# Two of three column blocks of the first expert, computed from the rows of the first 18 chunks by tasks of the attention's planner

## The chip, the cores and the metric

The kernel runs on one core of one Trainium2 chip. Its engines are TensorE (PE, with weight loads shown apart as PEld), VectorE (DVE), ScalarE (ACT), GpSimd (POOL) and SyncE (SP), which here only issues DMAs. The metric is the device time of one execution in microseconds. Everything is float32.

## The reference, cut to what matters

A delta-rule attention over 4 batches, 8 heads, 768 steps and 48 dimensions, whose output is the token matrix of a mixture of 8 experts with hash routing. Each token goes to one expert; there are 3072 tokens of 384 numbers, and an expert is two matrices, 384 by 1024 and 1024 by 384.

```python
for t in range(S):
    kt, vt, bt = (k_n[:, :, t], v[:, :, t], beta[:, :, t, None])
    y[:, :, t] = np.einsum('bhd,bhde->bhe', q[:, :, t], state)
    v_old = np.einsum('bhde,bhd->bhe', state, kt)
    state = state + bt[:, :, :, None] * np.einsum('bhd,bhe->bhde', kt, vt - v_old)
...
x = np.ascontiguousarray(attn_out.transpose(0, 2, 1, 3)).reshape(B * S, H * D)
expert_idx = token_ids * np.int64(2654435761) % np.int64(E)
for e in range(E):
    mask = expert_idx == e
    h = np.maximum(x[mask] @ w1[e], 0.0)
    out[mask] = h @ w2[e]
```

## The kernel before, in words

**Attention.** The 768 steps are cut into 24 chunks of 32 (`NU`, `C`); a chunk handles all 4 batches and 8 heads together. For groups of four chunks the kernel transposes keys and queries (`turn`, lines 381 to 395, into the four `KQ` tiles), multiplies them with each other (`gram`), and inverts the triangular systems on DVE (`inverse`, lines 494 to 554: 31 steps of two operations each), whose result `turn_back` transposes into `TU` (line 560). Then the chunks follow one another, because each needs the state S of the one before (`chunk`, line 594): `ask` reads the state with the keys and with the queries (line 581), R is V minus the first answer, `solve` applies the inverse (line 632), ACT copies the result to W (line 646), `update` adds to the state in PSUM (psS, line 653), the copies of `renew` bring S back to SBUF (lines 676 and 678), and `answer` completes y (line 689). `spread_t` and `masks_of` make the operands Tz and MT of a chunk (lines 466 and 472).

The last four chunks (`TAIL`, 20 to 23) are split in two halves of the heads, so that ACT and DVE share their work: there the eight copies of S are four on ACT (psS banks 0 and 1) and four on DVE (banks 2 and 3). Odd chunks of these four build y in PSUM bank z0, even ones in psY.

At a chunk's end ACT copies y to `x_sb` (line 698), and POOL writes its 128 rows to DRAM with an indirect DMA (`store`, lines 702 and 703). Each row goes to a place that is sorted by expert (`slot`), so that an expert's tokens lie one behind the other in `x_dram`.

**Who sets the order.** All attention work is recorded as tasks with a fixed duration, the names they read and write, and their engine (`task`, line 190). `order` (line 223) plays them through with these durations: an engine takes, of the tasks that are ready, the one with the longest chain of work behind it, plus its `boost`; `more` lengthens a chain, `hold` sets an earliest time, and `PATIENCE` tells how long an engine leaves itself idle for a more urgent task. A PSUM bank (`homes`: z0, z1, psX, psY and the four of psS) is given to a job by the same play. The result is written out as each engine's fixed instruction order.

**Routing.** On DVE, from the token ids: the expert of each token, its rank, the counts of each expert, and for every column block the rows to gather (`rows_i`), which of them are void (`none_f`), and a list of overflow blocks (`ov_i`), all in `routing` (line 717; its operations appear as line 728). The eight experts are sorted by their counts. An expert's own column blocks number `KTS` and hold `CWS` tokens each; what is over is done block by block in the last loop (line 1145). The inputs give no overflow block, before or after: the expert of place 4 has 376 tokens, 282 of them in the first 18 chunks.

**Experts.** They run in the order `RANKS`, place 4 first, which has three columns of 126. For a column, POOL gathers 128 rows (`gather`, line 1017), PE transposes them (`turn`, line 1036), DVE copies the result to xT (line 1038) and makes the token numbers (`token`, lines 1026 and 1028). `gemm1` (line 1044) makes eight blocks of h for all columns of an expert together, whose relu ACT and DVE take in turn (lines 1047 and 1049). `gemm2` (line 1060) makes the output of one column for experts with three columns; experts with four use `gemm2_turned` (line 1078) and turn the result back during the next expert's gemm1 (`send`, line 1088). The columns of the next expert are turned between. POOL scatters the output rows (line 1067).

Weights are 3 MB an expert. The first expert's are loaded in parts from SP behind the stores of the last chunks (lines 90 and 92); those of the next expert are issued from ACT after the first relu of each expert (`between`, lines 80 and 82).

## Time and profile before

Three runs took 538.76, 539.34 and 542.36 us, the median 539.34. The profile is one further execution:

| | |
|---|---|
| profiled execution | 532.51 us |
| its span, from first to last instruction | 530.9 us |
| PE busy | 476.5 us (90%) |
| DVE, ACT, POOL busy | 241.4, 185.9, 95.9 us |
| mean granted TensorE clock | 0.96 of full |
| DMA moved | 59.75 MB |

Stages: attention until about 234 us, then a seam of some 12 us, the experts from 246 to 520, and 11 us after the last scatter (519.7). Numbers of the profile are microseconds from the span's start, and durations are microseconds unless marked ns. A line of a timeline has start, length, engine, source line, operation, output and input tiles with their sizes, how many records were merged (x), and in brackets how long the engine had been idle before, and what it waited for. A window's line gives busy time for each engine, the clock granted to TensorE as a share of full speed, and the DMA engines' share and rate. Tile names are shown without buffer numbers. An f32 matmul leaves two records, a transpose one.

### The profile page before, as it was taken

Reading aid. Unit: us, or ns where it says so; the run is one execution under the profiler, and the core shown is the slowest. Engines: PE = TensorE matmul, PEld = TensorE weight load, DVE = VectorE, ACT = ScalarE, POOL = GpSimd, SP = SyncE. Lnnn points to the kernel's source line nnn. Section 1 sums busy time; section 2 is a strip of 40 time slices with the busy share of each in tenths; the row PEclk is TensorE's granted clock in tenths of the full one; section 3 lists DMA queues with packets and bytes.
Section 4 is the critical chain, followed back from the end, with each engine's and each line's share of the span. In section 5 each row is a group of like instructions: output and inputs, shape, how many; then the busy total and the mean of one; then the engine's idle time right before and its main releaser. Section 6 shows DMA issues by size and latency. Waiting matters only on the chain. (4 is left out here: it accounts for less than half of the span.)

```text
span 530.9 us, 15751 instructions
## 1 busy us (share of the span) xinstructions
PE 476.5 (90%) x6688; PEld 318.1 (60%) x6688; DVE 241.4 (45%) x775; ACT 185.9 (35%) x406; POOL 95.9 (18%) x139
## 2 busy tenths in 40 slices
PE   8865999998998898856999999999999999999990
PEld 5654677777777776643554555555655556565650
DVE  7697899998989886513110111211311111111100
ACT  4634779979796775320101101001011010101100
POOL 7000011021101122127013111302303021102010
PEclk9977899999999899986999999999999999999996
DMA  9959857575333437414705307107144071330000
GB/s 143 167 88 141 133 107 144 116 147 114 79 84 69 90 82 217 133 49 124 261 29 207 117 23 262 56 20 269 55 144 154 28 260 38 130 135 29 14 28 16
DMA packets 119128, 59.75 MB, mean 113 GB/s; under 512 B 104203, under 2 KB 112615, under 8 KB 119057
## 3 DMA queue, kind: packets, MB, share of 16 engines
q1 hardware_dynamic: 103664, 22.04, 23.5%
q10 hardware_dynamic: 10272, 22.14, 11.7%
q0 software_dynamic: 5120, 14.56, 7.9%
q8 instruction: 53, 0.87, 0.7%
q14 instruction: 19, 0.15, 0.1%
HBM read 49.90 MB, written 10.42 MB: 114 GB/s over the span
## 5 line engine op out<-in xcount | busy, mean ns | idle before, releaser
L1044 PE MATMUL h_ps<-xT,w_sb 128*128 128x378 f32 (+3 forms) x384 | 131.5, 496 | 4.0 <-DVE h_sb L1049 3.3
L1044 PEld LDWEIGHTS h_ps<-xT,w_sb 128*128 128x128 f32 x384 | 72.4, 192 | 56.0 <-issue 16.8
L1049 DVE TENSOR_SCALAR h_sb<-h_ps 128x378 f32<-128x378 f32 (+3 forms) x32 | 18.0, 563 | 151.6 <-PE h_ps L1044 151.6
L1078 PE MATMUL oT_ps<-h_sb,w_sb 128*128 128x424 f32 (+1 forms) x192 | 68.0, 507 | 0.0
L1060 PE MATMUL o_ps<-w_sb,h_sb 128*126 128x384 f32 (+1 forms) x192 | 63.6, 486 | 0.0
L546 DVE TENSOR_TENSOR tmp<-U,Ni 128x112 f32<-128x112 f32 (+15 forms) x186 | 61.6, 338 | 3.1 <-ACT U L530 0.4
L544 DVE TENSOR_TENSOR U<-U,tmp 128x112 f32<-128x112 f32 (+15 forms) x186 | 61.6, 338 | 3.0
L1067 POOL DMA_INDIRECT out_dram<-o_sb,idx_i x28 | 27.6, 986 | 194.1 <-ACT o_sb L1066 143.6
L703 POOL DMA_INDIRECT x_scratch<-x_sb,slot x24 | 25.0, 1043 | 193.7 <-DVE U L544 58.3
L1078 PEld LDWEIGHTS oT_ps<-h_sb,w_sb 128*128 128x128 f32 x192 | 35.5, 190 | 25.6 <-issue 13.9
L1047 ACT ACTIVATE h_sb<-h_ps 128x378 f32<-128x378 f32 (+3 forms) x32 | 15.8, 495 | 98.6 <-PE h_ps L1044 98.6
L1060 PEld LDWEIGHTS o_ps<-w_sb,h_sb 128*126 128x126 f32 (+1 forms) x192 | 35.0, 186 | 23.7
L676 ACT ACTIVATE S<-psS 48x384 f32<-48x384 f32 (+1 forms) x92 | 42.6, 463 | 17.4 <-PE psS L653 12.2
L1066 ACT COPY o_sb<-o_ps 126x384 f32<-126x384 f32 (+3 forms) x16 | 7.7, 478 | 83.5 <-PE o_ps L1060 69.0
L1017 POOL DMA_INDIRECT xg<-x_scratch,rows_i x28 | 28.2, 1007 | 34.4 <-DVE idx_i L1028 17.8
L653 PE MATMUL psS<-W,K 32*128 32x96 f32 x736 | 26.9, 280 | 5.8 <-ACT W L646 5.7
L1080 ACT COPY oT<-oT_ps 128x424 f32<-128x424 f32 (+1 forms) x8 | 4.0, 498 | 75.3 <-PE oT_ps L1078 75.3
L689 PEld LDWEIGHTS psY<-W,MT 64*64 64x64 f32 x704 | 23.3, 138 | 10.4 <-issue 9.1
L1038 DVE COPY xT<-xT_ps 128x318 f32<-128x318 f32 (+3 forms) x28 | 14.0, 499 | 33.7 <-PE xT_ps L1036 33.7
L653 PEld LDWEIGHTS psS<-W,K 32*128 32x128 f32 x736 | 22.8, 186 | 9.8 <-ACT W L646 8.3
L689 PE MATMUL psY<-W,MT 64*64 64x48 f32 x704 | 26.6, 225 | 0.0
L581 PE MATMUL psX<-S,KQ 128*32 128x96 f32 x672 | 23.0, 254 | 3.1 <-ACT S L676 2.2
(164 smaller groups left out, 590.9 us busy)
## 6 DMA issues: line engine op xcount, KB each, us to landing
w_sb<-in_moe_w_dram ACTq DMA_DIRECT2D x14, 1536.0 KB
Kt<-in_k_dram SPq DMA_DIRECT2D x24, 192.0 KB
Qt<-in_q_dram SPq DMA_DIRECT2D x24, 192.0 KB
V<-in_v_dram SPq DMA_DIRECT2D x96, 48.0 KB
K<-in_k_dram SPq DMA_DIRECT2D x96, 48.0 KB
w_sb<-in_moe_w_dram SPq DMA_DIRECT2D x3, 512.0 KB
w_sb<-in_moe_w_dram SPq DMA_DIRECT2D x4, 384.0 KB
xg<-x_scratch,rows_i POOLq DMA_INDIRECT x28, 3.0
```

Source lines behind the costliest of these rows:

```text
L544: nc.vector.tensor_tensor(U[:, n:, 0:n], U[:, n:, 0:n], t, op=ALU.add)
L546: nc.vector.tensor_tensor(t, U[:, j:n, 0:n].to_broadcast([P, m, n]), Ni[:, j, n:, None].to_broadcast([P, m, n]), op=ALU.mult)
L581: nc.tensor.matmul(res[quarter(b), u], lhsT=KQ[:, u, a, b, tk], rhs=S0[:, b, u].rearrange("p r d -> p (r d)"), start=(u == first and not o ...
L653: nc.tensor.matmul(psS[:, b, 2 * D * u:2 * D * u + 2 * D], lhsT=K4[quarter(b), u].rearrange("p r d -> p (r d)"), rhs=W[quarter(b), 2 * u:2 ...
L676: nc.scalar.activation(put, get, ACT.Copy)
L689: nc.tensor.matmul(py[rows, h], lhsT=MT[rows, h].rearrange("p e i -> p (e i)"), rhs=W[rows, h], start=(c == 0 and h == 0), stop=True, skip ...
L703: put = nc.gpsimd.indirect_dma_start(out=x_dram[:, :], out_offset=bass.IndirectOffsetOnAxis(ap=slot[:, c:c + 1], axis=0), in_=x_sb, in_off ...
L1017: nc.gpsimd.indirect_dma_start(out=xg, out_offset=None, in_=x_dram[:, :], in_offset=bass.IndirectOffsetOnAxis(ap=rows_i[:, c:c + 1], axis= ...
L1044: nc.tensor.matmul(h_ps[:, :width], lhsT=w1_sb[:, co, fo * P:(fo + 1) * P], rhs=xT[:, co, :width], start=(co == 0), stop=(co == CO - 1))
L1060: nc.tensor.matmul(o_ps[0:rows], lhsT=h_sb[:, fo, col * rows:(col + 1) * rows], rhs=w2_sb[:, fo, :], start=(fo == 0), stop=(fo == FO - 1))
L1067: scat = nc.gpsimd.indirect_dma_start(out=out[:, :], out_offset=bass.IndirectOffsetOnAxis(ap=idx, axis=0), in_=o_sb, in_offset=None, bound ...
L1078: nc.tensor.matmul(oT_ps[:, 0:width], lhsT=w2_sb[:, fo, i * P:(i + 1) * P], rhs=h_sb[:, fo, 0:width], start=(fo == 0), stop=(fo == FO - 1))
```

## The change

- `FIRST` is place 4, the expert that runs first; `SOON` is 18 chunks and `SC` two column blocks.
- **Rows of x in two parts.** Tokens of the first 18 chunks are ranked, by expert, in the first 2304 rows of `x_dram`, the others in the rest. The routing gets further operations: counts of both parts, the distance of an expert's second part from its first (`jump`), and a row number that jumps from one part to the other. Its last task has the priority `more` 75000 in place of 9000.
- **First expert.** The new `first_expert` adds tasks at the end of the list: two loads of its weights on SP; two gathers of 128 rows of the first part on POOL, which depend on the stores of chunks 0 to 17; their transposes, gemm1 for both columns at once (256 wide) and gemm2 on PE; relus and copies on ACT; token numbers on DVE. The PE tasks have a boost of -100000 and are `idle`: the engine waits longer for a more urgent task before it takes one of them. The remaining tokens of the expert, at most 128, form a third column that is done in the old place.
- **Memory.** The tiles `KQ2` and `KQ3` lie in two new tiles `wide`, which later hold the first expert's weights, xT and output; the four `Kt` tiles lie in `keys`, which later holds h.
- **The tail chunks.** y is always in psY, so z0 is free for the new tasks; psX and psS are freed for them after the last W. ACT's and DVE's copies of S are declared independent of each other (S copies freed).
- **Weights.** The second expert's take the place of the first's in the parts behind the last stores; the others are issued one expert earlier for the first three.
- **Built order.** On PE, the transposes of the first background column stand within chunk 20, between the halves of its first `ask`; those of the second column, and all background matmuls, stand behind the `answer` of chunk 23. The two gathers on POOL stand between the stores of chunks 17 and 18. The token numbers on DVE stand before R of chunk 20.

```diff
-    CWS = [106, 106, 98, 98, 126, 126, 121, 121]
+    CWS = [106, 106, 98, 98, 128, 126, 121, 121]
...
+    FIRST = RANKS[0]
+    SOON, SC = 18, 2
...
+    wide = [first.tile([P, 4096], F32, name=f"wide{i}") for i in range(2)]
+    keys = first.tile([P, 2048], F32, name="keys")
+    w1_first = wide[0][:, 0:CO * F].rearrange("p (co f) -> p co f", co=CO)
...
+    xT_first = wide[0][:, CO * F:CO * F + CO * SC * P].rearrange("p (co x) -> p co x", co=CO)
+    o_first = wide[1][:, FO * DIN:FO * DIN + SC * DIN].rearrange("p (k d) -> p k d", k=SC)
+    h_first = keys.rearrange("p (fo x) -> p fo x", fo=FO)
...
+        KTs = [keys[:, i * 512:i * 512 + 512].rearrange("p (u r d) -> p u r d", u=HU, r=2)
+               for i in range(B)]
...
+        KQs = tiles(2, "KQ", [P, HU, 2, B, NB]) + [
+            t.rearrange("p (u a b x) -> p u a b x", u=HU, a=2, b=B) for t in wide]
...
                 soon = [x for x, i in r
-                        if at < x < at + PATIENCE * tasks[pick]["ns"] and rest[i] > rest[pick]]
+                        if at < x < at + (1.0 if tasks[pick]["idle"] else PATIENCE)
+                        * tasks[pick]["ns"] and rest[i] > rest[pick]]
...
+                for b in t["release"]:
+                    banks[b] = end[pick] + LAG[e]
...
-            split, odd = c >= TAIL, c >= TAIL and c % 2 == 1
+            split = c >= TAIL
...
-            yb, yn = (zs[0], "z0") if odd else (psY, "psY")
-            yc = ((0,), ()) if c == TAIL + 1 - TAIL % 2 else ((), ())
+            yb, yn, yc = psY, "psY", ((), ())
...
+            over = ((len(zs), *range(len(zs) + 2, len(homes))), (1,)) if c == NU - 1 else ((), ())
...
+                         W[:, hs.start:hs.stop], pws[i][:, hs.start:hs.stop], ACT.Copy),
+                     release=over[i])
...
-                                    nc.scalar.activation(put, get, ACT.Copy)
+                                    copy = nc.scalar.activation(put, get, ACT.Copy)
                                 else:
-                                    nc.vector.tensor_copy(put, get)
+                                    copy = nc.vector.tensor_copy(put, get)
+                                if split:
+                                    tc.declare_no_dep(copy.ins, group=f"renew{c}{1 - q}",
+                                                      reason="other banks, other places")
+                                    tc.add_to_no_dep_group(f"renew{c}{q}", copy.ins)
...
+            W1, LATER = E * SOON, NTC - SOON
+            sides = ((slice(0, W1), slice(0, SOON)), (slice(W1, W), slice(SOON, NTC)))
+            for side, cs in sides:
+                n = cs.stop - cs.start
+                dv("tensor_tensor", oh[:, side].rearrange("p (e c) -> p e c", e=E),
+                   eid[:, None, cs].to_broadcast([P, E, n]),
+                   iota_f[:, 0:E, None].to_broadcast([P, E, n]), op=ALU.is_equal)
...
+            for side, cs in sides:
+                dv("tensor_reduce", r[:, cs],
+                   rank_f[:, side].rearrange("p (e c) -> p c e", e=E), axis=AX.X, op=ALU.add)
...
+            dv("tensor_tensor", soons, ends1, start, op=ALU.subtract, reads=("rt",), **on)
+            dv("tensor_tensor", key, ahead[:, W1 + LATER:W + 1:LATER], start2, op=ALU.subtract,
+               **on)
+            dv("tensor_tensor", key, key, soons, op=ALU.add, **on)
+            dv("tensor_tensor", more, start2, ends1, op=ALU.subtract, **on)
...
+            for what, to in ((one_e, which), (key, cnt), (start, begin), (soons, early),
+                             (more, jump)):
...
+            for to, what in ((own_bgn, begin), (own_erl, early), (own_jmp, jump)):
+                dv("tensor_copy", to, what[:, :, None].to_broadcast(EK), **on)
...
             for what, to, sign in ((first, frm[:, E * KT:], 1.0), (left, lim[:, E * KT:], -1.0),
-                                   (which, ovf[:, 0:NOV], 0.0)):
+                                   (begin, bgn[:, E * KT:], 0.0), (early, erl[:, E * KT:], 0.0),
+                                   (jump, jmp[:, E * KT:], 0.0), (which, ovf[:, 0:NOV], 0.0)):
...
             dv("tensor_scalar", out=none_f, in0=lim, scalar1=row_f, scalar2=float(BIG),
                op0=ALU.is_le, op1=ALU.mult, **on)
-            dv("scalar_tensor_tensor", out=frm, in0=frm, scalar=row_f, in1=none_f,
-               op0=ALU.add, op1=ALU.max, **on)
-            dv("tensor_copy", rows_i, frm, more=9000, **on)
+            dv("scalar_tensor_tensor", out=erl, in0=frm, scalar=row_f, in1=erl,
+               op0=ALU.add, op1=ALU.is_ge, **on)
+            dv("tensor_tensor", jmp, jmp, erl, op=ALU.mult, **on)
+            dv("scalar_tensor_tensor", out=frm, in0=frm, scalar=row_f, in1=bgn,
+               op0=ALU.add, op1=ALU.add, **on)
+            dv("tensor_tensor", frm, frm, jmp, op=ALU.add, **on)
+            dv("tensor_tensor", frm, frm, none_f, op=ALU.max, **on)
+            dv("tensor_copy", rows_i, frm, more=75000, **on)
...
+        def first_expert():
+            def weights(i, w, into, out):
+                def go():
+                    if not i:
+                        which_first.append(expert_at(FIRST, mybir.EngineType.SP))
+                    src = w[bass.ds(which_first[0], 1)].rearrange("o a b -> (o a) b")
+                    n = out.shape[1]
+                    src = src.rearrange("(o p) x -> p o x", p=P)
+                    for at in range(0, n, n // (3 + i)):
+                        nc.sync.dma_start(out=out[:, at:at + n // (3 + i)],
+                                          in_=src[:, at:at + n // (3 + i)])
+                task("SP", 2500, ("lim",), tuple(
+                    f"KQ{2 + i}{a}{b}" for a in range(2) for b in range(B)) + (into,), go,
+                    kb=600)
+            which_first = []
+            weights(0, moe_w1, "w1", w1_first)
+            weights(1, moe_w2, "w2", w2_first)
+            for k in range(SC):
+                c = FIRST * KT + k
+                def fetch(k=k, c=c):
+                    got = nc.gpsimd.indirect_dma_start(
+                        out=xg_tiles[k], out_offset=None, in_=x_dram[0:SOON * P, :],
+                        in_offset=bass.IndirectOffsetOnAxis(ap=rows_i[:, c:c + 1], axis=0),
+                        bounds_check=SOON * P - 1, oob_is_err=False)
+                    tc.add_to_no_dep_group("rows", got.ins)
+                task("POOL", 1100, tuple(f"x_dram{i}" for i in range(SOON)) + ("lim",),
+                     (f"xg{k}",), fetch, kb=200)
+                job = new_job(1, early=True)
+                def turn_rows(k=k, job=job):
+                    for co in range(CO):
+                        nc.tensor.transpose(bank(job)[:, co * P:(co + 1) * P],
+                                            xg_tiles[k][:, co * P:(co + 1) * P], ident)
+                task("PE", 450, (f"xg{k}",), (f"j{job}",), turn_rows, words=6, job=(job, 0),
+                     idle=True, boost=-1e5)
+                task("ACT", 500, (f"j{job}",), (f"xT{k}",), lambda k=k, job=job:
+                     nc.scalar.activation(
+                         xT_first[:, :, k * P:(k + 1) * P],
+                         bank(job)[:, 0:DIN].rearrange("p (co x) -> p co x", co=CO), ACT.Copy),
+                     job=(job, 0))
+                def number_of(k=k, c=c):
+                    f, i = idx_first[k]
+                    nc.vector.tensor_tensor(f, xg_tiles[k][:, DIN:DIN + 1], none_f[:, c:c + 1],
+                                            op=ALU.max)
+                    nc.vector.tensor_copy(i, f)
+                task("DVE", 220, (f"xg{k}", "lim"), (f"idx{k}",), number_of)
+            for fo in range(FO):
+                job = new_job(1, early=True)
+                for co in range(CO):
+                    task("PE", 440, ("w1", "xT0", "xT1"), (f"j{job}",),
+                         lambda fo=fo, co=co, job=job: nc.tensor.matmul(
+                             bank(job)[:, 0:SC * P], lhsT=w1_first[:, co, fo * P:(fo + 1) * P],
+                             rhs=xT_first[:, co], start=(co == 0), stop=(co == CO - 1)),
+                         words=2, job=(job, 0), idle=True, boost=-1e5)
+                task("ACT", 370, (f"j{job}",), (f"h{fo}",), lambda fo=fo, job=job:
+                     nc.scalar.activation(h_first[:, fo], bank(job)[:, 0:SC * P], ACT.Relu),
+                     job=(job, 0))
+            for k in range(SC):
+                job = new_job(1, early=True)
+                for fo in range(FO):
+                    task("PE", 660, ("w2", f"h{fo}"), (f"j{job}",),
+                         lambda fo=fo, k=k, job=job: nc.tensor.matmul(
+                             bank(job)[:, 0:DIN], lhsT=h_first[:, fo, k * P:(k + 1) * P],
+                             rhs=w2_first[:, fo], start=(fo == 0), stop=(fo == FO - 1)),
+                         words=2, job=(job, 0), idle=True, boost=-1e5)
+                task("ACT", 490, (f"j{job}",), (f"o{k}",), lambda k=k, job=job:
+                     nc.scalar.activation(o_first[:, k], bank(job)[:, 0:DIN], ACT.Copy),
+                     job=(job, 0))
...
+            first_expert()
...
-                    w_tiles[0], parts = load_w_parts(
-                        expert_at(RANKS[0], mybir.EngineType.SP), w_pool)
+                    w_tiles[1], parts = load_w_parts(
+                        expert_at(RANKS[1], mybir.EngineType.SP), w_pool)
...
-    with tc.tile_pool(name="w_pool2", bufs=3) as w_pool2, \
...
+        def send_rows(rows, idx, alone):
             scat = nc.gpsimd.indirect_dma_start(
                 out=out[:, :], out_offset=bass.IndirectOffsetOnAxis(ap=idx, axis=0),
-                in_=o_sb, in_offset=None, bounds_check=N - 1, oob_is_err=False)
+                in_=rows, in_offset=None, bounds_check=N - 1, oob_is_err=False)
...
+            for kt in range(SC if e == FIRST else 0, KTS[e]):
                 xgs[e * KT + kt] = gather(e * KT + kt, next(gathered))
...
-            for kt in range(KTS[RANKS[0]]):
-                turn_one(RANKS[0], kt)
+            for k in range(SC):
+                send_rows(o_first[:, k], idx_first[k][1], True)
+            turn_one(FIRST, SC, 0)
...
-                    if fo == 0 and len(rest) > 0:
-                        w_tiles[i + 1] = load_w(expert_at(rest[0], mybir.EngineType.Activation),
-                                                w_pool if i == 3 else w_pool2, nc.scalar)
+                    to = i + 2 if i < 2 else i + 1
+                    if fo == 0 and to < E and to not in w_tiles:
+                        w_tiles[to] = load_w(
+                            expert_at(RANKS[to], mybir.EngineType.Activation),
+                            w_pool if to == 4 else w_pool2, nc.scalar)
...
-                gemm1(w1_sb, xTs.pop(e), h_sb, CAPS[e], between)
+                gemm1(w1_sb, xTs.pop(e), h_sb, CAPS[e] if i else P, between)
...
-                        gemm2(w2_sb, h_sb, j, CWS[e], idx[e * KT + j], True)
+                        if e != FIRST:
+                            gemm2(w2_sb, h_sb, j, CWS[e], idx[e * KT + j], True)
+                    if e == FIRST:
+                        gemm2(w2_sb, h_sb, 0, P, idx[e * KT + SC], True)
```

## The prediction

> **What bounds the kernel now.** I read the page's slices first, then stages, the chain of waits, and the order of time at the seam between attention and experts. The named chain that ended last is of no use here: it stops at the last scatter.
>
> Stages at the seam (us, then busy time of PE, PEld, DVE, ACT, POOL, granted clock, DMA share, GB/s):
>
> ```profile
> core 0: us, PE busy (x) PEld busy (x) DVE busy (x) ACT busy (x) POOL busy (x), PEclk, DMA share, GB/s
> 227.00:234.00 7.00, 6.49 (x182) 5.09 (x176) 2.13 (x6) 2.45 (x7) 1.17 (x2) 1.00 0.10 36
> 234.00:242.00 8.00, 0.06 (x2) 0.00 (x0) 1.89 (x5) 0.49 (x1) 3.53 (x4) 0.59 0.19 57
> 242.00:247.00 5.00, 3.43 (x11) 2.04 (x12) 2.31 (x9) 0.00 (x0) 3.78 (x5) 0.50 0.48 138
> ```
>
> TensorE is the bound nearly everywhere, except from 234 to 242, where it has nothing to do, and then it restarts at half its clock. The waits of 206 to 247 (total, times, longest) name the reason, and a second loss in the four split chunks:
>
> ```profile
> PE xT_ps L1036 <- DMA xg<-x_scratch,rows_i: 8.8, 3, 8.0
> DVE S L678 <- ACT S L676: 8.8, 12, 2.6
> ACT S L676 <- DVE S L678: 3.9, 9, 0.5
> ```
>
> The first expert's rows can be gathered only once the last chunk's rows are in DRAM. In order of time on PE (start, length):
>
> ```profile
> 232.74 1.31 PE L689 MATMUL z<-W,MT 64*64 64x48 f32 x32
> 242.10 0.86 PE L1036 MATMUL xT_ps<-ident,xg 126*128 126x126 f32 x3 [8.04 <-DMA xg<-x_scratch,rows_i]
> ...
> 246.19 9.27 PE L1044 MATMUL h_ps<-xT,w_sb 128*128 128x378 f32 x24 [0.69 <-DVE idx_f L1026]
> ...
> 280.47 8.70 PE L1044 MATMUL h_ps<-xT,w_sb 128*128 128x424 f32 x24
> ```
>
> So from the last attention matmul (234.05) to the second expert's first (280.47) pass 46.4 us: 8.0 idle, 4.1 turning three columns, 17.6 gemm1, 16.6 gemm2 with four turned columns between. A logical f32 matmul is two records ("x24" is 12). Warm prices come from later:
>
> ```profile
> 436.06 3.98 PE L1044 MATMUL h_ps<-xT,w_sb 128*128 128x378 f32 x12
> 439.87 0.49 PE L1088 MATMUL o_ps<-ident,oT 128*98 128x128 f32 x3
> ...
> 445.99 5.33 PE L1060 MATMUL o_ps<-w_sb,h_sb 128*126 128x384 f32 x16
> 451.16 0.47 PE L1036 MATMUL xT_ps<-ident,xg 121*128 121x121 f32 x3
> ```
>
> 3.81 us for 6 matmuls of 378 columns, 1.68 ns a column; 5.17 us for 8 of 384, 0.646 each. Finally the S copies of chunk 20, ACT's and DVE's taking turns:
>
> ```profile
> 213.71 0.32 ACT L676 ACTIVATE S<-psS 48x192 f32<-48x192 f32 x1 [1.55 <-PE psS L653]
> 214.52 0.33 ACT L676 ACTIVATE S<-psS 48x192 f32<-48x192 f32 x1 [0.48 <-DVE S L678]
> ...
> 216.36 0.36 DVE L678 COPY S<-psS 48x192 f32<-48x192 f32 x1 [0.39 <-ACT S L676]
> ```
>
> **What the skill says.** "TensorE: Matmul & The Clock Gate", Part 1: an idle window of about 3.4 us drops the array to half clock, a busy one restores it. The trace agrees: 8.0 us idle, then 0.50 granted, and gemm1 takes 17.6 us where four times 3.81, 15.2 us, is its warm time. "PSUM — Partial Sum Buffer", Engine vs sequencer instructions: ScalarE, VectorE and GpSimd queues are strict FIFO and matmuls start in program order. So a task that waits for a gather holds all that stands behind it; here DVE's copies wait in turn, as shown. Same page, PSUM bank collisions: accesses of two engines to different banks are clean. ACT reads psS banks 0 and 1, DVE 2 and 3, so the copies can overlap; no run here shows it. "DMA: Bandwidth & Descriptors", Anatomy of one DMA: about 2.0 us fixed plus bytes over 436 GB/s, an estimate of 2.5 us for 205 KB of rows. The trace has 3.26 us (gather starts 238.84, its transposes 242.10), which I use.
>
> **The change, part by part.** The built order tells what the diff doesn't: on PE only the transposes of column 0 stand inside chunk 20. Those of column 1, all 24 gemm1 and all 16 gemm2 matmuls of the background stand behind the last chunk's answers. So the work isn't in the chunks' gaps; it fills the idle 8 us and keeps the clock up.
>
> *Seam.* From the last answer: (a) the x copy and the xT copy on ACT, 0.1 + 0.49 + 0.49 and a handover of 0.2, until gemm1 can start: 1.3 (column 1's transposes, 0.5, lie inside). (b) 24 matmuls of 256 columns at 1.68 ns: 10.3. (c) 16 of 384: 10.3. (d) the third column: TensorE's register load of n_ov (0.49 before, in the idle time, now partly seen: 0.3), transposes 0.5, DVE copy 0.55 with handover, no cover: 1.4. (e) 24 matmuls of 128 columns: 5.2, plus 0.6 because ACT issues two weight loads (250.68 to 251.69) between its relus of 128 columns and two h_ps banks then run out: 5.8. (f) four columns of the second expert now turned in one go, paced by DVE (264.50 to 265.15, 0.65 each; two banks), gemm2 behind them: 2.0. (g) 8 of 384: 5.2. Sum 36.3 against 46.4: **10.1 us saved**. The third gather is hidden: chunk 23's rows are stored near 235.4 and gathered near 242, while (b) and (c) run to about 256. Unknown is (e): no 128-column stream with fresh weights is in the trace. Lower end 5.2; upper, the LDWEIGHTS record of 190 ns for each of 48, unoverlapped, 9.1. I take 5.8, since three 128-column transposes with fresh weights take 0.49 together. The two o copies and scatters are off PE; on POOL the scatters stand ahead of the third expert's gathers, which nobody needs for another 20 us.
>
> *S copies.* Before, the last of eight ends 3.0 us after the first starts, the fourth after 1.5. Side by side four take about 1.5 (two 0.75). So half of chunk 21's S arrives 0.8, the other 1.5 us earlier. The ask, R and solve follow: solve came 4.2 us behind the first copy (217.89), now about 3.2, since PE's own asks (four of 0.54) then bind, and MT on DVE (0.69). 1.0, 1.0 and 0.8 for the three updates: **2.8 saved**; ends 1.5 (only the late half counts) and 4.5 (all of it). What is late next is PE. That y always uses psY costs nothing while the x copy (0.49) follows S's on ACT at +2.0, about when asks for y begin.
>
> *Routing on DVE.* About 20 more operations, 6.3 us by durations. But interleaved with the inverse's chain they mostly vanish: U of 207 elements steps 0.41 with a small rt between and 0.41 without. Only the wide ones show: 97.17 to 97.79 instead of 0.45 (+0.17), 98.97 to 99.67 (+0.24). Three added pairs: 1.3. The built order also puts V1 of chunk 21 ten operations ahead of the last inverse's end, where it stood behind it; that is some 3.5 us later against the chunks. Tz of chunk 20 ended at 203.8 and solve needed it at 210.0, so most of it is covered; DVE's queue up to R then ends near 210, R stood at 209.25: **1.0 added**, ends -1 and 5.
>
> *Gathers and weights.* Two gathers on POOL between stores 17 and 18: 198.04 + 3.43 (as from 235.41 to 238.84) = 201.5, 1.3 each, done 203.9; store 18 comes at 204.42. They land at 204.8 and 206.1. Behind them on DVE stand R of chunk 20 and its MT, on PE the second half of chunk 20's ask (near 209): 3 us of cover; a later landing is paid one for one. The transposes cost 0.3 in chunk 20. The first expert's 3 MB on SP's queue wait for the same chunks (11 and 15) as the K loads behind them; 7 us at the 216 GB/s seen from 213 to 220, against two chunks (13 us) until that K is used: nothing. The second expert's loads take the old place, and all later experts load one expert earlier.
>
> Sum: -10.1 - 2.8 + 1.0 + 0.3 = -11.6. Span 530.9 gives 519.3, the execution 532.51 gives 520.9. The median of runs, 539.34, stands 6.8 above that execution; I carry the difference: **527.7 us**.
>
> **Rivals.** (1) *The copies give little.* PE is busy 6.49 of 7.00 in the last chunk, which speaks for it; that a psS wait of 1.55 stands in each, against. With 1.5 for S and (e) at its upper end, +4.6: 532.3. (2) *More is gained*, S at 4.5 and no DVE delay: 525.0 to 523. (3) *The gather is late*: DVE and PE stand in chunk 20; 8 us beyond landing as above, less 3 of cover, give 532.7. Against it: weights of the next expert, issued at 203.07 before, now come a chunk later. (4) *Slower*: the last inverse binds. Place: its transpose (201.17) ahead of Tz and solve of chunk 20. If routing cost its 6.3 us in full and grams of that group slipped two chunks (7.8 each between stores 7 and 15), less 6 of cover, 15.9 us would be added in place of 1.0: 542.6. It decides once the transpose ends more than 6 us later against chunk 19, and turns the sign at about 18. For it: DVE is above 95% busy from 80 to 120. Against: the order differs by one chunk, not two. (5) *It doesn't do what it says*, no background in the chunks: that is my reading, and it is in the sum.
>
> **How the numbers follow.** Forecast as worked out (525 to 531): 0.58; (1) 0.18; (2) 0.12; (3) 0.07; (4) 0.05. The range 523.5 to 533.5 leaves out most of (4), part of (3) and the edge of (2). About 1%, 5.4 us, is what a measurement can tell here: faster 0.88 (forecast, (2), nearly all of (1), half of (3)), within 1% 0.08, slower 0.04.
>
> **What would show it.** PE never idle over 2 us near the seam, clock 1.0 throughout; from the last attention matmul to the 424-column gemm1 36 us; S copies on ACT and DVE with equal starts; split chunks near 6.2 us instead of 7.4; the transpose of the last inverse not over 206. I am wrong if PE stands before the transposes of column 0 or R of chunk 20, or if the last attention matmul ends after 236.

## The result and the profile after

The changed kernel took 532.54 us (median of five runs, 529.57 to 534.16) against 539.34 (on record five runs too, 538.76 to 542.36): 0.9857 of before, 95% interval 0.9813 to 0.9901. This ratio and those below compare fast runs alone, and are not quotients of the medians beside them (here 0.9874). The kernel is faster, by 6.8 us where 11.6 were forecast; 532.5 lies in the range of 523.5 to 533.5, but above the 525 to 531 that the forecast itself gave. Its profiled execution took 529.57 us with a span of 528.0 and a mean clock of 0.976 (before: 532.51, 530.9, 0.96). So the two profiled executions differ by 2.9 us only, less than half of what the medians differ by. That had to be understood first.

The stages at the seam of the changed kernel (us, busy time of PE, PEld, DVE, ACT, POOL, granted clock, DMA share, GB/s), on three stretches like those shown of before:

```profile
core 0: us, PE busy (x) PEld busy (x) DVE busy (x) ACT busy (x) POOL busy (x), PEclk, DMA share, GB/s
230.00:237.00 7.00, 6.93 (x206) 5.84 (x204) 2.13 (x6) 3.00 (x9) 1.17 (x2) 1.00 0.13 44
237.00:245.00 8.00, 6.95 (x40) 5.26 (x37) 1.89 (x5) 1.67 (x4) 3.31 (x4) 1.00 0.16 51
245.00:250.00 5.00, 4.96 (x19) 3.29 (x19) 0.00 (x0) 0.77 (x2) 2.71 (x3) 1.00 0.49 137
```

TensorE works through the eight us behind the last answers, 6.95 where it worked 0.06, and at full clock where it had half. The waits of 206 to 247 no longer have ScalarE's and VectorE's copies of S waiting for each other; both wait for TensorE alone:

```profile
ACT S L701 <- PE psS L678: 5.3, 4, 1.8
DVE S L703 <- PE psS L678: 5.3, 3, 3.5
```

TensorE in order of time from the last answers to the second expert (start, length, in brackets the idle time before and what ended it):

```profile
236.18 1.14 PE L718 MATMUL psY<-W,MT 64*64 64x48 f32 x32
...
238.37 1.13 PE L993 MATMUL psX<-wide 128*128 128x256 f32 x4 [0.58 <-ACT wide L977]
...
242.56 0.70 PE L993 MATMUL psS<-wide 128*128 128x256 f32 x2 [0.47 <-ACT keys L998]
...
261.79 0.55 PE L1175 MATMUL xT_ps<-ident,xg 128*128 128x128 f32 x3 [0.58 <-ACT wide L1009]
263.10 3.00 PE L1183 MATMUL h_ps<-xT,wide 128*128 128x128 f32 x24 [0.77 <-DVE idx_f L1165]
266.71 2.37 PE L1183 MATMUL h_ps<-xT,wide 128*128 128x128 f32 x18 [0.61 <-issue]
270.30 0.94 PE L1183 MATMUL h_ps<-xT,wide 128*128 128x128 f32 x6 [1.22 <-DVE h_sb L1188]
...
273.07 5.34 PE L1199 MATMUL o_ps<-wide,h_sb 128*128 128x384 f32 x16
278.25 1.23 PE L1183 MATMUL h_ps<-xT,w_sb 128*128 128x424 f32 x3
```

The seam, from 237.32 to 278.25, takes 40.9 us instead of 46.4. The gain is 5.5, not 10.1; and the attention ends at 237.32, which the prediction had named as a sign of being wrong (later than 236), and 3.3 us later than before. At first sight the change lost time on some 100 us of attention in which it does nothing but more routing. The experiments show that most of this was no effect of the change.

### The profile page after: what moved, and what is told of

It is laid out like the page before. It is cut to its first block, busy times and chain, and to the rows that moved or that the text cites. A ratio compares the mean times of both kernels' runs of the same rounds, so it can differ in the third digit from the quotient of the medians.

```text
span 528.0 us, 15909 instructions
## 1 busy us (share of the span) xinstructions
PE 478.9 (91%) x6736; PEld 324.6 (61%) x6736; DVE 239.0 (45%) x797; ACT 190.0 (36%) x417; POOL 97.1 (18%) x141
## 3 DMA queue, kind: packets, MB, share of 16 engines
q10 hardware_dynamic: 8832, 19.00, 10.2%
## 5 line engine op out<-in xcount | busy, mean ns | idle before, releaser
L1183 PE MATMUL h_ps<-xT,w_sb 128*128 128x424 f32 (+3 forms) x336 | 114.2, 493 | 2.3 <-DVE h_sb L1188 2.3
L1183 PEld LDWEIGHTS h_ps<-xT,w_sb 128*128 128x128 f32 x336 | 62.7, 190 | 46.8 <-issue 14.6
L1188 DVE TENSOR_SCALAR h_sb<-h_ps 128x424 f32<-128x424 f32 (+4 forms) x32 | 17.0, 530 | 142.1 <-PE h_ps L1183 142.1
L1199 PE MATMUL o_ps<-w_sb,h_sb 128*121 128x384 f32 (+1 forms) x144 | 47.6, 486 | 0.0
L1186 ACT ACTIVATE h_sb<-h_ps 128x424 f32<-128x424 f32 (+4 forms) x32 | 15.0, 469 | 79.4 <-PE h_ps L1183 77.0
L1199 PEld LDWEIGHTS o_ps<-w_sb,h_sb 128*121 128x121 f32 (+1 forms) x144 | 26.2, 185 | 18.1
L1205 ACT COPY o_sb<-o_ps 106x384 f32<-106x384 f32 (+4 forms) x15 | 7.2, 478 | 74.0 <-PE o_ps L1199 59.6
L1177 DVE COPY xT<-xT_ps 128x318 f32<-128x318 f32 (+4 forms) x26 | 12.9, 494 | 45.3 <-PE xT_ps L1175 45.3
L655 PE MATMUL psX<-R,Tz 64*64 64x48 f32 x672 | 27.6, 221 | 5.0 <-issue 3.2
L718 PEld LDWEIGHTS psY<-W,MT 64*64 64x64 f32 x768 | 24.8, 134 | 10.1 <-issue 8.2
L655 PEld LDWEIGHTS psX<-R,Tz 64*64 64x64 f32 x672 | 23.5, 134 | 9.7 <-issue 5.2
```

The source lines that it names most:

```text
L655: nc.tensor.matmul(pws[i][rows, h], lhsT=Tz[rows, h].rearrange("p e i -> p (e i)"), rhs=R[rows, h], start=(h == (hs.start if split else 0) ...
L718: nc.tensor.matmul(py[rows, h], lhsT=MT[rows, h].rearrange("p e i -> p (e i)"), rhs=W[rows, h], start=(c == 0 and h == 0), stop=True, skip ...
L1183: nc.tensor.matmul(h_ps[:, :width], lhsT=w1_sb[:, co, fo * P:(fo + 1) * P], rhs=xT[:, co, :width], start=(co == 0), stop=(co == CO - 1))
L1199: nc.tensor.matmul(o_ps[0:rows], lhsT=h_sb[:, fo, col * rows:(col + 1) * rows], rhs=w2_sb[:, fo, :], start=(fo == 0), stop=(fo == FO - 1))
```

## The experiments

The runs came in three sets (s, t, u). A set has one chip (the record numbers them 6, 3 and 6), and runs of the kernel before beside it; before's own median differs from set to set. Ratios are to before in the same set:

| run | median us (n) | before in its set | ratio (95% interval) |
|---|---|---|---|
| s1, copies alone | 535.3 (11) | 539.7 | 0.9893 (0.9863 to 0.9923) |
| s2, before with more on DVE | 541.03 (20) | 539.7 | 1.0017 (0.9995 to 1.0039) |
| s3, late loads | 531.99 (4) | 539.7 | 0.9850 (0.9780 to 0.9919) |
| s4, routing on POOL | 534.37 (14) | 539.7 | 0.9880 (0.9847 to 0.9913) |
| t1, before again | 534.33 (20) | 534.16 | 1.0015 (0.9990 to 1.0040) |
| t2, serial copies | 524.23 (4) | 534.16 | 0.9827 (0.9763 to 0.9890) |
| t3, late gathers | 530.61 (13) | 534.16 | 0.9919 (0.9886 to 0.9951) |
| t4, plain order | 523.25 (4) | 534.16 | 0.9796 (0.9721 to 0.9872) |
| u1, changed kernel again | 523.51 (6) | 535.44 | 0.9781 (0.9737 to 0.9824) |
| u2, serial copies again | 523.40 (6) | 535.44 | 0.9785 (0.9755 to 0.9816) |
| u3, copies alone again | 529.73 (6) | 535.44 | 0.9892 (0.9853 to 0.9932) |
| u4, third column early | 525.66 (6) | 535.44 | 0.9817 (0.9786 to 0.9848) |

And what one profiled execution of each shows, in us: from the store of chunk 0's rows to that of chunk 17's; from there to the end of the last answers; the seam; the rest of the span behind it. The last column is where, from 60 to 290 us, the granted clock fell to 0.9 or less (stretches of 5 us, by their starts). What lies ahead of the store of chunk 0 is left out; it takes 67.5 to 71.5 us, and differs as much between two profiles of one program (before 70.3 and 67.5, changed 68.6 and 70.8).

| | store 0 to 17 | to last answers | seam | rest | clock fell at |
|---|---|---|---|---|---|
| before, as predicted from | 127.8 | 36.0 | 46.4 | 250.4 | 180, 235 to 245 |
| t1 before again | 126.0 | 36.0 | 47.8 | 250.6 | 230 to 245 |
| s1 copies alone | 131.6 | 34.0 | 47.0 | 250.6 | 235 to 245 |
| u3 copies alone | 129.6 | 31.4 | 47.7 | 250.6 | 180 to 185, 235 to 245 |
| s2 before, more DVE | 135.4 | 38.1 | 46.8 | 250.5 | 95 to 105, 245 to 255 |
| changed kernel | 132.0 | 36.7 | 40.9 | 249.8 | none |
| u1 changed again | 126.0 | 37.0 | 39.2 | 249.7 | 225 to 230 |
| t2 serial copies | 126.3 | 36.3 | 39.2 | 249.7 | none |
| u2 serial copies | 126.1 | 36.3 | 39.1 | 249.7 | none |
| s3 late loads | 132.1 | 38.4 | 39.6 | 249.7 | 225 to 230 |
| s4 routing on POOL | 134.6 | 39.5 | 40.9 | 249.7 | 95 to 105, 235 to 240 |
| t3 late gathers | 125.9 | 42.2 | 39.1 | 249.7 | 210 to 220 |
| t4 plain order | 125.8 | 36.7 | 39.4 | 249.7 | 225 to 230 |
| u4 third column early | 128.0 | 39.7 | 38.9 | 249.7 | 170 to 175, 220 to 230 |

**s1 and u3, the S copies alone.** The edit, in the kernel before:

```diff
-                                    nc.scalar.activation(put, get, ACT.Copy)
+                                    copy = nc.scalar.activation(put, get, ACT.Copy)
                                 else:
-                                    nc.vector.tensor_copy(put, get)
+                                    copy = nc.vector.tensor_copy(put, get)
+                                if split:
+                                    tc.declare_no_dep(copy.ins, group=f"renew{c}{1 - q}",
+                                                      reason="other banks, other places")
+                                    tc.add_to_no_dep_group(f"renew{c}{q}", copy.ins)
```

> The kernel before with one part of the change alone: the split chunks' S copies on ScalarE and VectorE no longer wait for each other; every instruction keeps its place on its engine. On record I put the gain at 2.8 us, in chunks 20 to 22 (1.0, 1.0, 0.8). Read from the changed kernel's trace, where the way from chunk 20's first S copy to the last answers got 2.0 us shorter: 2.0. Theory: last attention matmul at about 232.0 instead of 234.05, time 536.5 to 537.5 against 539.3. Rival (the copies were behind TensorE's work anyway, and the shorter way in the changed kernel is due to other parts): under 0.7 us, 539.

> The kernel before with the S copies free and nothing else, a second time: it makes the square of before, copies alone, the rest alone and the whole on one chip. Theory: 0.986 to 0.993 of before, as the first time (0.9893). Rival (that gain was another chip's, where TensorE has longer stalls): 0.995 to 1.0.

Both times the copies alone gave 1.1%. From store 17 to the last answers it takes 31.4 us in u3 and 36.0 in t1, 4.6 less, where the prediction had counted 2.8; within the set s it is 34.0 in s1 and 38.1 in s2, 4.1 less. The theory held, with a larger price (its 232.0 for the last answers did not: they end at 234.8 in s1, since that set is later by store 17 already). From the store of chunk 19 to those of chunks 20, 21, 22 and 23 it takes 5.55, 5.84, 5.08 and 3.53 us in u3, and 6.82, 7.39, 6.56 and 3.85 in t1. The Trainium skill ("PSUM — Partial Sum Buffer", PSUM bank collisions) says that accesses of two engines to different banks run clean; here the copies run side by side at almost their old speed. ScalarE and VectorE in u3, four copies each, 0.34 and 0.37 us a copy; they took 0.32 to 0.36 when they took turns:

```profile
214.77 1.37 ACT L676 ACTIVATE S<-psS 48x192 f32<-48x192 f32 x4 [1.55 <-PE psS L653]
```

```profile
214.81 1.48 DVE L678 COPY S<-psS 48x192 f32<-48x192 f32 x4 [0.88 <-PE psS L653]
```

**s2, more work on VectorE before.**

```diff
...
+                def go():
+                    getattr(nc.vector, name)(*[a() if callable(a) else a for a in args], **kw)
+                    if on == "lim":
+                        lims[0] += 1
+                        if lims[0] <= 20:
+                            nc.vector.tensor_tensor(spare, zero, zero, op=ALU.add)
...
```

> The kernel before with 20 additions of two 128x32 tiles of zeros, one behind each of the first 20 VectorE instructions of the routing's second part, into a tile that nobody reads; no other instruction moves. The changed kernel's routing takes 20.4 us of VectorE where before's takes 14.7. The additions take 0.16 to 0.25 us each by the rows of like size, 3.2 to 5 us together, between 95 and 150 us. Theory (VectorE, 93% busy from 60 to 205 us, sets the pace, and the 5.7 us more of routing are what made the attention end later than forecast): the last inverse is finished later by the whole sum, the last attention matmul by 60 to 100% of it, 237 to 238 instead of 234.05; time 542 to 544. Rival (the new order on the engines, not VectorE's work, made it late): last attention matmul 234 to 235, time 539 to 540.

The twenty took 0.19 us each, 3.7 together, and cost 0.17% (-0.05 to 0.39%), 0.9 us. But they did not land where the expectation put them: the first twenty operations of that part stand early, nineteen between 11.6 and 40 us and one at 84.1, not between 95 and 150. From store 5 to store 17 this kernel takes 93.2 us, and the copies alone, without additions, 93.2 as well. So it says only that VectorE has room early on. Where the routing stands is decided below, by u1 against t1.

**s3, the weight loads behind the relus.**

```diff
-                    if fo == 0 and to < E and to not in w_tiles:
+                    if fo == (0 if i else FO - 1) and to < E and to not in w_tiles:
...
-                    elif fo == 1 and len(rest) > 1:
+                    if fo == 1 and len(rest) > 1:
```

> The changed kernel, with the two weight loads that ScalarE issues in the first expert's third column put behind the last of its four relus there (they stood behind the first); nothing else moves. In the changed kernel's trace the third column's first matrix product takes 8.0 us where 24 products of 0.217 take 5.2, and two relus come after the issues (0.43 and 0.81 us). Theory (the issues hold the relus back, the relus the PSUM banks): 8.0 becomes 6.0 to 6.6, second expert's first product 1.4 to 2.0 earlier (276.3 to 276.9 instead of 278.25), time 530.5 to 531.2 against 532.5. Rival (the relus' own way from TensorE to ScalarE and back sets it, or an instruction fetch of TensorE, the gap of 0.61 us at 266.7): under 0.5 us earlier.

TensorE in s3, the third column's first matrix:

```profile
267.06 5.26 PE L1183 MATMUL h_ps<-xT,wide 128*128 128x128 f32 x42 [0.76 <-DVE idx_f L1165]
272.83 0.94 PE L1183 MATMUL h_ps<-xT,wide 128*128 128x128 f32 x6 [0.51 <-DVE h_sb L1188]
273.60 0.71 PE L1175 MATMUL xT_ps<-ident,xg 106*128 106x106 f32 x6
```

267.06 to 273.60 are 6.54 us, 1.4 less than 8.0, and the seam is 39.6 instead of 40.9: as the theory had it. In the time it doesn't show, since the changed kernel alone has an interval that wide. In the later sets the unedited kernel needs 6.2 to 6.3 us there, so that most of those 1.4 us were a loss of the first set alone.

**s4, a part of the routing on GpSimd.** Thirteen VectorE operations become twenty on GpSimd; the first of the edits:

```diff
-                     lambda: getattr(nc.vector, name)(
+                     lambda: getattr(by, name)(
                          *[a() if callable(a) else a for a in args], **kw), more=more, job=job)
...
+                by, it = (nc.gpsimd, got_p) if to is jump else (nc.vector, got)
```

> The changed kernel with 13 of the routing's VectorE instructions done by GpSimd instead (20 there, reductions as trees of additions); all of TensorE's, ScalarE's and SyncE's instructions and the rest of VectorE's keep their order. It takes some 3.0 us off VectorE between 95 and 150 us. Theory (VectorE's work makes the attention late): last inverse's transpose at 204.9 instead of 207.86, last attention matmul 2 to 3 us earlier (233 to 234 instead of 236.2), time 530 against 532.5. Rival (the order makes it late): under 0.7 us earlier; if GpSimd's twenty instructions stand in the way of the x rows or of VectorE's memory port: later by up to 2 us.

The theory fell. From store 5 to 17 it takes 92.7 us where the changed kernel takes 93.4 and s3 93.2: at most 0.7 less for 2.7 us less of routing on VectorE (18.5 instead of 21.3). The time is not better (0.9880). Nor did VectorE keep its pace: beside GpSimd's two operations on 128x176 numbers, its own of that size took 0.82 and 0.83 us instead of 0.45. So this run alone doesn't acquit VectorE's routing; t1 and u1 below do.

**t1, before once more.** No edit.

> The kernel before, unchanged, profiled once more, to know how much of the trace's differences any other run of the same kernel shows. Its first profiled execution, 532.51 us, lies under all 40 later ones (537.14 to 544.2), and two kernels with the same order of instructions, the S copies alone and the additions, needed 38.3 and 42.2 us from the store of chunk 0's rows to that of chunk 5's where it needed 35.95 (the changed kernel: 38.6). Theory: the first profile of before was a short draw; the new one shows 38 us or more for chunks 0 to 5, and the last answers end at 236.5 to 239 instead of 234.05, so that the changed kernel's 237.3 is no loss against it. Rival: 36 us and 234 again, and the changed kernel did lose 3.3 us by the end of the attention.

Here the rival was right, and then not in the way it meant. From store 0 to store 5 the kernel before needs 36.0 us again, and from store 17 to the last answers 36.0, the same chunk by chunk. But the changed kernel in this set and the next needs the same 36: from store 0 to 17 t1 takes 126.0, t2 126.3, t4 125.8, u1 126.0 and u2 126.1. In the set s and in the result's own profile it takes 131.6 to 132.1, with the order of before (s1) as with the changed one, as long as the clock stays up. So the profile of before behaves like the sets t and u and the profile of after like the set s, and **the 4.2 us that the attention seemed to lose up to store 17 are a difference between two sets of runs, not between two kernels**. GpSimd's stores of chunks 0 and 17 in the changed kernel, first profile:

```profile
68.61 1.19 POOL L732 DMA_INDIRECT x_scratch<-x_sb,slot  x1 [56.30 <-ACT MT L496]
...
200.60 0.98 POOL L732 DMA_INDIRECT x_scratch<-x_sb,slot  x1 [5.15 <-ACT R L641]
```

and in u1, the same program:

```profile
70.84 1.22 POOL L732 DMA_INDIRECT x_scratch<-x_sb,slot  x1 [58.18 <-ACT MT L496]
...
196.80 0.98 POOL L732 DMA_INDIRECT x_scratch<-x_sb,slot  x1 [5.14 <-ACT R L641]
```

In the changed kernel's first profile TensorE stood 17.2 us before its weight loads, for nothing that the profile shows, between 68 and 200 us; in u1, the same program, 13.3. Why the sets differ stays open; s and u have the same chip number. And routing and the new order cost nothing there: from store 5 to 17 t1 takes 90.0 us and u1 90.0, with 6.1 us more of routing on VectorE (21.8 us in all instead of 15.7).

A second use of t1: its profiled execution, 529.58 us, is the shortest of its 20, and 4.7 under their median. A profile may be a short draw, as that of before was.

**t2 and u2, the copies waiting again in the changed kernel; u1, the changed kernel beside it.** The edit takes the five lines of s1 out again.

> The changed kernel with its S copies waiting for each other again in the split chunks; every instruction keeps its place. Alone on top of the kernel before the free copies were worth 1.07% (0.79 to 1.37%), 4.2 to 7.4 us, and 4.1 us in the trace between two kernels at full clock. Theory (the copies stand between one chunk's update and the next chunk's products with S, whatever else was changed): taking them away costs the same here, 3 to 5 us, 535.5 to 537.5 against 532.5; chunks 20 to 22 each 1.0 to 1.4 us longer. Rival (the rows' transposes that stand in these chunks fill the wait): under 1.5 us.

> The changed kernel with its S copies waiting for each other, a second time, now beside the changed kernel itself. Its four executions before gave 0.9827 (0.976 to 0.989), no worse than the changed kernel's own 0.9857 on another chip. Theory (the parts add): 0.980 to 0.988, and slower than the changed kernel by 0.8 to 1.3%. Rival (the clock takes the copies' gain): equal to the changed kernel within 0.4%.

> The changed kernel itself, on the same chip as the three beside it. Theory (the parts add): the free copies are worth 0.8 to 1.3% beside before, the rest (columns in the background, routing, rows in two parts) 1.2 to 2.0%, so that the whole is 2.0 to 3.2% faster than before, ratio 0.968 to 0.980. Rival (they don't add: with the copies free TensorE stands less in the split chunks, and its clock then falls to half there, as in four of the five changed kernels profiled with free copies after the first): the whole is no faster than the rest without the copies, ratio 0.980 to 0.986.

The parts don't add. With the rest of the change the free copies give nothing: 0.9781 with, 0.9785 without, both with intervals of some 0.4%. Where does the gain go? TensorE in chunk 22 with free copies, u1:

```profile
221.85 0.43 PE L655 MATMUL psX<-R,Tz 64*64 64x48 f32 x6
223.81 0.49 PE L655 MATMUL psX<-R,Tz 64*64 64x48 f32 x9 [1.54 <-issue]
...
224.78 1.84 PE L678 MATMUL psS<-W,K 32*128 32x96 f32 x32
226.55 1.94 PE L718 MATMUL psY<-W,MT 64*64 64x48 f32 x32
```

and with copies that wait, u2:

```profile
223.38 1.04 PE L655 MATMUL psX<-R,Tz 64*64 64x48 f32 x15
...
224.94 1.17 PE L678 MATMUL psS<-W,K 32*128 32x96 f32 x32
226.04 1.14 PE L714 MATMUL psY<-W,MT 64*64 64x48 f32 x32
```

The free copies bring TensorE to the solve 1.5 us earlier (221.85 against 223.38). It begins, stops in the middle of it for 1.54 us for nothing that the profile shows, and comes to the update at 224.78 against 224.94. The whole lead is gone. Then it works at half clock, and the update takes 1.84 us instead of 1.17. The stages of u1 and of u2:

```profile
217.00:221.00 4.00, 3.52 (x96) 3.00 (x96) 2.77 (x6) 2.12 (x6) 0.00 (x0) 1.00 1.03 308
221.00:224.00 3.00, 1.46 (x52) 1.14 (x46) 0.98 (x3) 0.00 (x0) 1.17 (x2) 1.00 0.68 247
224.00:231.00 7.00, 7.00 (x148) 6.38 (x148) 2.13 (x6) 2.45 (x7) 1.15 (x2) 0.57 0.02 5
```

```profile
221.00:224.00 3.00, 2.27 (x68) 1.57 (x60) 2.02 (x5) 0.89 (x3) 0.90 (x1) 1.00 0.29 109
224.00:231.00 7.00, 6.17 (x170) 5.04 (x170) 2.13 (x6) 2.66 (x8) 1.19 (x3) 1.00 0.09 34
```

All seven profiles of a changed kernel with free copies have this stop in the same solve, ahead of the same instruction, of 0.6 to 2.3 us (s3 0.63, the first profile 0.98, t3 1.22, u1 1.54, t4 1.80, s4 1.81, u4 2.33). Neither of the two with copies that wait has it, nor any of the five with the order of before, free copies or not.

What TensorE waits for there is its own program. Each trace lists, packet by packet, 53 transfers of 16 KB on a DMA queue that the profile calls "instruction" (packets, MB, share):

```profile
q8 instruction: 53, 0.87, 0.7%
```

That is one for about 256 of the 13,582 instructions recorded for TensorE in u1. In all seven profiles TensorE goes on 2.3 to 2.5 us after the start of such a transfer (u1: 221.34 and 223.81; u4: 225.87 and 228.18). In u2 the transfer starts at 221.39, as in u1, but TensorE comes to that instruction later and stands 0.12 us. So the lead that the copies give ends where the next instructions arrive. The place 256 instructions earlier, in chunk 21's update, has a stop too in four of the seven, 0.28 us in the first profile, 0.48 in u1, 1.05 in s3 and 1.37 in u4, which the view puts down to K:

```profile
220.33 1.21 PE L681 MATMUL psS<-W,K 32*128 32x96 f32 x26 [1.37 <-DMA K<-in_k_dram]
```

It also ends 2.6 to 2.8 us after the start of such a transfer, so K or the instructions may have come last.

Why the transfer starts so late is not shown. Counted from when TensorE began the 256 instructions before, it starts 3.0 to 5.5 us later in all nine changed kernels. The second expert's weights, which SyncE issues at 208 and 215 us in u1, fill the DMA engines then: the share is 1.03 up to 221 in u1 and has fallen to 0.29 when u2 comes to the solve. But the kernels with the order of before load as much, the first expert's, about a chunk earlier; at shares of 0.85 to 1.04 their transfers start 1.2 to 2.9 us later and TensorE stands 0.12 us at most. And in u4 the share is down to 0.34 from 223 and 0.13 from 225, yet the transfer starts at 225.87. No run moves the weights away, so that they are the cause is argued and not shown. In six of the seven the clock falls in chunks 20 to 22, in none of the two: after this stop in u1, s4 and t4, after the one in chunk 21's update in s3, at both in u4, and in t3 well ahead of either. That the stops bring the clock down isn't shown.

**t3, the gathers behind store 18.**

```diff
                 tc.declare_no_dep(put.ins, group="rows", reason="disjoint rows")
                 tc.add_to_no_dep_group("rows", put.ins)
+                if c == SOON:
+                    for go in held:
+                        go()
...
-                     (f"xg{k}",), fetch, kb=200)
+                     (f"xg{k}",), lambda fetch=fetch: held.append(fetch), kb=200)
```

> The changed kernel with GpSimd's two gathers of the first expert's rows put behind the store of chunk 18's rows (they stand before the copy of that chunk's row numbers); nothing else moves. In the changed kernel the gathers wait 3.3 to 3.8 us for chunk 17's rows to land, the copy of the numbers stands behind them, ScalarE's copy of chunk 18's rows waits for that copy, and ScalarE's next copy, of R, releases TensorE's solve; from store 17 to store 18 it takes 8.4 to 8.9 us in three kernels with the gathers there and 6.4 to 6.9 in three without. Theory (the queue of GpSimd): store 17 to 18 takes 6.4 to 7.1 us, last answers 1.5 to 2 us earlier after store 17 (34.8 instead of 36.7), time 530.5 to 531. Rival A (two stutters of TensorE of 0.4 us each, which wait for nothing that the profile shows, set it, and come with the gathers' traffic): these move with the gathers, and the same 1.5 us are lost one chunk later; time 532 to 533. Rival B (the rows now come too late for column 0's transposes in chunk 20): loss of 1 us or more there.

Rival B, and dearer than it said. From store 17 to 18 it takes 6.4 us, as the theory had it, but chunk 20 then waits. TensorE in t3:

```profile
210.63 0.90 PE L974 MATMUL z<-ident,xg 128*128 128x128 f32 x3 [4.15 <-DMA xg<-x_scratch,rows_i]
```

TensorE and VectorE both stand 4.15 us for the rows, then the clock is 0.50 from 210 to 220, and from store 19 to 20 it takes 13.7 us instead of 6. So the cover of these gathers is real, and it is thin: in the built order they are in time, and a little later they cost 7 us. In the sets t and u there was nothing to win by it anyway: stores 17 to 19 are 12.8 us apart in t1 and in u1 alike, since chunk 19 takes back what chunk 18 loses. In the first set the changed kernel needed 15.2 there and the copies alone 13.7; there the gathers do seem to cost 1.5. The way is the one that the expectation names, in the changed kernel's first profile on GpSimd and on ScalarE:

```profile
204.84 1.04 POOL L959 DMA_INDIRECT xg<-x_scratch,rows_i  x1 [3.26 <-DVE tmp L570]
206.18 1.00 POOL L959 DMA_INDIRECT xg<-x_scratch,rows_i  x1 [0.30 <-issue]
207.19 0.22 POOL L731 COPY x_sb<-number 128x1 f32<-128x1 f32 x1
```

```profile
207.76 0.49 ACT L727 ACTIVATE x_sb<-psY 128x384 f32<-128x384 f32 x1 [1.57 <-remote]
```

The first gather stands 3.26 us in GpSimd's queue, the copy of chunk 18's row numbers behind it, and ScalarE's copy of the rows waits for that.

**t4, the background's products in plain order.**

```diff
                          words=2, job=(job, 0), idle=True, boost=-1e5)
...
-                         words=2, job=(job, 0), idle=True, boost=-1e5)
+                         words=2, job=(job, 0), idle=True, boost=-2e5)
```

> The changed kernel with the two columns' 24 products of the first matrix all before the 16 of the second (they stood mixed); ScalarE's relus follow. In the changed kernel the 40 products take 22.8 us where 24 of 0.431 and 16 of 0.645 take 20.7; two stalls of 0.47 wait for ScalarE's relu to free a PSUM bank, and each change from one matrix to the other leaves about 0.1 to 0.2. Theory (the mixed order brings the stalls): the 40 take 21.3 to 21.8 us with one wait of 0.5 to 0.7 at the change, seam 1 to 1.5 us shorter, time 531 to 531.5. Rival (the stalls come from the plan's choice of banks whatever the order, or the end, where both output copies come together, is what counts): seam 40.5 to 41.2 as before.

The theory fell: 235.07 to 257.8 are 22.7 us, as in the mixed order, now with these two stalls and one of 0.96 ahead of the third column:

```profile
239.26 1.56 PE L993 MATMUL psS<-wide 128*128 128x256 f32 x6 [0.47 <-ACT keys L998]
241.30 1.56 PE L993 MATMUL psS<-wide 128*128 128x256 f32 x6 [0.47 <-ACT keys L998]
```

The built order tells why. The product at 242.56 in the first profile writes the third bank of psS and waits for a relu that reads the first; the one at 256.54, with the other gap of 0.47, writes the fourth, and its relu reads the first as well. psS is one tile of four banks, and a write to one waited here for an earlier read of another, the same kind of wait that the change had taken from the S copies. That t4's two gaps are of this kind is likely, and no run took these waits away.

**u4, the third column turned early, and the loads of s3.** The core of the edit (a gather, three transposes and their copies as further background tasks):

```diff
+            task("POOL", 1100, tuple(f"x_dram{i}" for i in range(NU)) + ("lim",), (f"xg{SC}",),
+                 fetch_third, kb=200)
...
+            task("PE", 450, (f"xg{SC}",), (f"j{job}",), turn_third, words=6, job=(job, 0),
+                 idle=True, boost=-5e4, slack=4000)
+            task("ACT", 900, (f"j{job}",), ("xT_third",), keep_third, job=(job, 0))
```

> The changed kernel with two edits at the seam: the third column's rows are gathered and turned as background work too, between the 40 products of the first two columns, and ScalarE's two weight loads stand behind the third column's relus. In the changed kernel it takes 1.9 us from the last of the 40 products to the third column's first product (0.58 for the output copies, 0.5 for the transposes, 0.77 for VectorE's copy of them), and 6.2 us on one chip and 8.0 on another to run its 24 products. Theory: the 1.9 becomes 0.3 to 0.7 and the 24 products take 6.2 to 6.6; the 3 transposes add 0.4 among the 40; seam 37.5 to 38.5 instead of 39.2 to 40.9, time 0.2 to 0.45% under the changed kernel's. Rival (the output copies hold the PSUM banks that the third column's products need, and the register load stands there too): the 1.9 stays over 1.2, seam over 38.7, no difference in the time that can be measured.

TensorE in u4, the turning in the background, and the third column's start:

```profile
253.60 0.49 PE L1005 MATMUL psS<-ident,xg 128*128 128x128 f32 x3
253.93 0.60 PE L1019 MATMUL psS<-wide 128*128 128x256 f32 x2
255.24 0.70 PE L1019 MATMUL psS<-wide 128*128 128x256 f32 x2 [0.71 <-ACT wide L1010]
...
263.81 0.71 PE L1209 MATMUL h_ps<-wide 128*128 128x128 f32 x4 [0.58 <-ACT wide L1035]
```

The step between background and third column shrank to 0.7 us, and its 24 products took 5.8, as wished. But the transposes went into psS, and the next product waited for their copy: the background grew from 22.7 to 24.0. Net 0.3 us of seam, and no gain in the time. No kernel of these is measurably faster than the changed one.

## Why the prediction was right, and where it was wrong

**Sign and mechanism.** Right. The gain comes from the seam: TensorE is no longer idle for eight us and its clock no longer falls there. In all five profiles with before's seam the clock fell to 0.5 there, for some 14 us between 233 and 261; in none of the nine with the new seam did it. In the set u the kernel is 2.2% faster (11.9 us), in its own 1.4%.

**Seam, "36.3 against 46.4".** The direction held and the sum was too good, in the forecast's own steps:

| step | forecast | first profile | u1 |
|---|---|---|---|
| (a) copies before gemm1 | 1.3 | 1.05 | 1.05 |
| (b)+(c) 40 products | 20.6 | 22.7 | 22.7 |
| (d) third column turned | 1.4 | 2.05 | 2.05 |
| (e) 24 products of 128 | 5.8 | 7.97 | 6.30 |
| (f) 12 transposes | 2.0 | 2.00 | 1.99 |
| (g) 8 of 384 | 5.2 | 5.18 | 5.18 |
| sum | 36.3 | 40.9 | 39.2 |

The terms that were mis-sized: (b) and (c) were priced as products alone, without the 2.1 us of gaps between them, two of 0.47 waiting for relus; (d) left out the 0.58 for the output copies; and (e) was 0.5 too small in the later sets and 2.2 in the first, within the two ends given. Within one set the seam shrinks from 47.0 to 40.9 (s) and from 47.7 to 39.2 (u): 6.1 and 8.5 us saved, not 10.1. Behind the seam another 0.7 to 0.9 us were saved that no step had (rest 249.7 instead of 250.5).

**S copies, "2.8 saved".** The mechanism was right, its price too low when alone (4.1 to 4.6 in the traces, 1.1% in time), and the step failed in the sum: with the rest it is zero. "What is late next is PE" stopped one thing short. Late next were TensorE's own instructions in chunk 22, which the sum has at nothing. So it has the second expert's weights, the candidate for why they come late: "The second expert's loads take the old place", without a price. Their first part doesn't take quite that place: SyncE issues it 3.8 us after the store of chunk 18 in u1 (208.23 and 204.45), and 1.3 us ahead of that store in u3 (204.16 and 205.47), with the order of before.

**Routing, "1.0 added".** Shown to be nothing: 90.0 and 90.0 us from store 5 to store 17 in like sets, with 26 more operations of 5.5 to 6.1 us. The reasoning was right that small operations vanish between the inverse's chained ones; the wide pairs vanish too.

**Gathers, "3 us of cover".** Right, and t3 shows what lies behind: 4.15 us of standing and then half clock, some 7 us in one chunk. What was overlooked is the queue that they stand in. GpSimd's copy of the row numbers waits behind them and with it ScalarE, 1.5 us in one set and none in the others.

**From profile to median, "I carry the difference".** Before's profile was a short draw, 6.8 under its median; the changed kernel's stood 3.0 under its own. Within the first set the steps as measured are seam -6.1, rest -0.8, copies 0, routing 0, gathers 1.5: -5.4, and the medians say -6.8 (5.3 to 10.1 by the interval). In the set u they are -8.5 and -0.9: -9.4, and the medians say -11.9 (9.4 to 14.1). So the sum of the steps closes at the edge of what was measured, with 1.4 and 2.5 us that I can't place. That the copies are worth nothing was measured in the later sets only. The forecast's 11.6 fits the set u, but by two errors that cancel: the copies' 2.8, which aren't there, and these 2.5 us.

**The rivals.** The time came out at the first rival's 532.3, which had (e) at its upper end (9.1; measured 8.0) and half of the copies' gain (measured none). The fourth, that the last inverse binds, decides only when its transpose is over 6 us late against chunk 19; it came 7.3 us after store 17 where it came 3.1 after, 4.1 later, and TensorE waited for no Tz in chunk 20. Two of the prediction's own signs of being wrong did come: this transpose after 206 (207.86), 2.6 us of it with the set and 4.1 with the new order, and the last answers after 236, which in u1 end at 233.8.

## What to carry to other kernels

A gain from taking a wait away is a gain in when the next instruction is reached, and it lasts only if the instructions behind it and their data are there earlier too; price it again after moving transfers, by the whole and by the parts alone. A tile of several PSUM banks that two engines share brings waits between banks that have nothing to do with each other; count them for each new user of the tile. And compare two traces stage by stage only with a run of the old kernel from the same set beside them: here 4 us of "loss" in an untouched stage were a difference between sets.
